# ScalarE is allowed to take the weights' low words, and every step gets a new place and a new engine choice

## The chip, the cores and the metric

The kernel runs on one core of one Trainium2 chip. The metric is device microseconds (us) of one execution; the figure shown is the median of three runs. The engines are TensorE (PE, with its weight loads as PEld), VectorE (DVE), ScalarE (ACT), GpSimd (POOL) and SyncE (SP), which issues nearly all DMAs.

## The reference

Attention over 8 batch elements, 8 heads, 576 positions and 64 channels. All scores that lie more than tau under the maximum of their row are dropped before the softmax. A gated feed-forward layer follows, which mixes each position with the one before it:

```python
scores = scale * np.matmul(q, k.transpose(0, 1, 3, 2))
scores = np.where(scores >= np.max(scores, axis=-1, keepdims=True) - tau, scores, -1e9)
attn = softmax(scores); x = np.matmul(attn, v)      # heads side by side: 8 x 576 x 512
xk = mu_k * x + (1 - mu_k) * x_prev; xr = mu_r * x + (1 - mu_r) * x_prev
out = sigmoid(xr @ w_r) * (np.maximum(xk @ w_k, 0.0) ** 2 @ w_v)
```

The three weight matrices arrive as 64-bit floats (512x1024, 1024x512 and 512x512).

## The kernel before, in words

**Jobs and units.** A job is a pair of heads of one batch element. There are 36: the first batch element is cut into two halves (jobs 0 to 7), and each later batch element has four jobs (8 to 11, 12 to 15 and so on). A job has up to four units of two times 128 query rows and one unit for the last 64 positions. For every block of 128 rows and 576 keys, `softmax` makes four steps: PE writes the scores to PSUM (tile `s`, two of them); DVE takes the negated maximum of each row (L740); a small step derives the row's threshold (L748 on ACT, L756 on DVE or L761 on POOL); ACT takes the exponential (L768); DVE masks it by the threshold and sums it (L776). The block is then turned (by PE at L830 for the early jobs, by DVE and DMA for the later ones), copied out of PSUM by `evict` (L845 on ACT or L846 on DVE), and multiplied by v in `attend` (PE, L1017). I call this last step a job's product.

**Feed-forward.** When all jobs of a batch element are done, `ffn_chunk` handles 256 positions at a time: L1211 (xk by w_k), L1262 (xr by w_r) and L1285 (squared activations by w_v) on PE, with ACT, POOL and DVE steps between them.

**Weights.** `weight` turns each of the 20 pieces of 128x512 64-bit floats (8 of w_k, 4 of w_r, 8 of w_v) into 32-bit floats, and then into a high and a low part. POOL clamps the high words (L444), and ACT scales them into a buffer (L451). DVE shifts the low words right by 29, which leaves three bits, and writes these to a PSUM tile (L459). DVE ors the sign in (L467), and shifts the buffer left by three and ors the PSUM tile in (L477). A copy on ACT or POOL makes the high part (L487 or L491) and POOL subtracts it (L496).

**Order.** No loop and no planner run on the chip. The kernel text adds 5647 steps in program order. A table of two-character digits, PLACES, gives each step its place, and a string, PICKS, gives one digit to each step that may run on several engines. The steps are issued in the order of the table, so each engine has a fixed queue and waits at each instruction for what it needs. 21 steps of dummy transposes on PE (L1378) are among them. PSUM holds two score tiles `s` and four general tiles `w`, and the low words' bits use one of these four.

Of the kernel before, what the change touches and what calls it, by code (L numbers as in the profile page):

```python
# [22 lines left out]
    "!(!!!$!#!+!,!o%x!*!)!%!&!1!=!r!}$0$C$>$G$^%C%m!.!c!n#)#1#=#E#H!w#g$U&)&9&](Z(t!2!]#G#Q#a#w$M&>!0#b&4(*(9(B(S(~#+#m#v",  # L23
    "&p&y(%(z)+!`&Q)&)1)H)^*,*7#@$B(`(b(p({*(*A#L$;)w*4*D*N*T*b%[&J)s)f)y*%*9*Z!f$)*B*S*d*n*v*{$E&~*Y*y*~+)+0+8$])j*x+.+3",
    "+A+K+R!e#>+G+E+T+e-<-H$?&[,|.1.A.N.q/$#4$F+p,C,Q,X.E/Y%d(0+c+[+o+|,*,=(l+`-a-N-i-u-~.)#Z.4/T/M/]/e/j/o*)-e0$0*060<0G",
    "0L!-!P#l!>!<!C!E!F!Q!?!A!B!D!S!V!x#!!_!k!X!q!^#&!T!O![!b!d!j!U!W!Y!a!l!~#3#8!s##!y#(#-#0#:#I#N#d#h#p!@#,$Z!i!m!p!u!t",
    "!z!v!|!{#%#*#D#M#O#<#B#6#J#T#[#$#.#/#7#2#9#5#C#;#F#W#}$1$:$!$+#j#s#R#Y$J$N$O$S$V$[!/!R%W#A#U#K#V#P#X#`#f#c#i#{#~$I$T",
    "#n#x$($5$2$@#r#_#z$%$#$-#e#q#k#u$8$=$z$~$g$x$,$<$`$c%,%2%4%F%K%c!Z#?&<#S#]#t$9$4#|#o$$$.$6#y$D$K$H$P$&$3$/$7$Y${%+%B",
    "$p$t$l%8$k$n$A$X$L$R$Q$W$b$i$h$o%b%o%|&!$r%$%&%:%=%N&,&/&1&6&:&K$_%3%U%g*K%9%I%V&c()(8(^)T)q(J(i)S){*0*6*=*F*L*Q*U*W",
    "*e+D+m+r,),1,4,:,k,o,r,{-:-@.:.T*@*J*O*]*a*g*q*z+,+w-k.v-v-z-}.+.U.^.c.e.m.w/</C+4+;+>+M+V*u*|+(+C+Q,Y/Q/_/b/h0P0^0b",  # L30
    "1E1L1_0y0}1%11191G1u1{2%2T$*$e(3$m$w$}%#%(%E%S%@%L$a$d$f$j$s$q$u%7%<%M%]%f&$%}%j%p%s$v$y$|%%%!%-%*%0%)%1%.%5%?%G%P%_",
    "%r&&%T%`&E&G%>%D%6%;%H%X%R%Y%A%O%J%Q%n%v&i&l%l%w%~&?%e%k&x(#(&(-(/(T(Y%/%h))%{&+&0&H&X&T&2&8&B%Z%^%a%i%u%q%z&C&N&R&`",
    "&Z&g&d&k&n&u%t%y&%&(&#&*&-&3&.&5&7&=&f($(1(6&A&U&M&_&h&t&;&@&F&I&D&S&L&V&P&Y&W&b&q&z(A(X&{(2&s&|(](d(o(s(y(|)%);)=&O",
    "(()z(.(5(<(C(H(M(=(W(e&^&a&e&j&r&w(+(Q(v)>)L(I).(n(E(K(L(4(7&m&o(>(D(F(N&v&}(!(,(m(u)#),(_(g(:(?(j(x(V(a(;(@(h(q(r)$",
# [263 lines left out]
def tile_threshold_attention_then_rwkv_ffn(  # L298
# [17 lines left out]
    P = 128  # L316
# [94 lines left out]
    def weight(j, name, w, c, f, key, wait):  # L411
# [8 lines left out]
        def t():  # L420
            return xT[1].get()[:, col, 1 : 1 + 512]
# [7 lines left out]
        def high():  # L429
# [1022 lines left out]
```

## Time and profile before

| | us |
|---|---|
| median of 3 runs | 916.03 (915.87 to 916.19) |
| the profiled execution's own time | 915.72 |
| its span, first to last instruction | 914.0 |
| DMA busy share in the window from 75 to 150 us | 0.40 |

Busy time is the union of an engine's instruction intervals. PE's intervals are modelled and overlap, so a full row of PE does not mean that PE runs at its peak. A number of the form x24 counts instructions. The granted clock is full over the whole span in the page's slices.

### The profile page before, as it was taken

The page shows a single profiled execution, that of the slowest core. Times are in us where ns is not written, and L with a number is a line of the kernel's source. Part 1 is how long each engine was busy: PE and PEld are TensorE (multiplying, and loading weights), DVE is VectorE, ACT ScalarE, POOL GpSimd, SP SyncE. Part 2 cuts the span into 40 slices and gives each one's busy share as a digit, 9 for nine tenths or more (in the row PEclk, how much of TensorE's full clock was granted, in tenths as well). Part 3 has the DMA queues.
Part 4 walks back from the last instruction along what each step waited for, and adds up shares of the span by engine and source line. Part 5 has one row for each costly group of instructions (what it writes and reads, how often), then busy time and mean ns, then how long its engine had stood idle before and what let it go on. Part 6 is the DMA issues. An engine that isn't in the chain of part 4 may idle for free.

```text
span 914.0 us, 17624 instructions
## 1 busy us (share of the span) xinstructions
PE 902.3 (99%) x5970; PEld 744.1 (81%) x5970; DVE 715.5 (78%) x1615; ACT 598.5 (65%) x1154; POOL 666.5 (73%) x824
## 2 busy tenths in 40 slices
PE   8999999999999999999999999999999999999997
PEld 6677877797878887988887978888889888879986
DVE  7999999998878898988889988888888777701131
ACT  6789999778675767565755475757686666434211
POOL 1789988886774967786977686867687868577742
PEclk9999999999999999999999999999999999999999
DMA  8767333499989999899987979999898887630001
GB/s 332 276 217 246 105 106 119 145 305 308 334 296 311 313 320 322 301 323 313 299 297 272 315 252 321 305 321 320 296 321 291 281 310 261 238 131 24 24 24 23
DMA packets 146249, 226.60 MB, mean 248 GB/s; under 512 B 20080, under 2 KB 82672, under 8 KB 146160
## 3 DMA queue, kind: packets, MB, share of 16 engines
q1 hardware_dynamic: 146016, 225.49, 73.1%
q8 instruction: 47, 0.77, 0.4%
q14 instruction: 42, 0.34, 0.1%
q10 hardware_dynamic: 144, 0.00, 0.0%
HBM read 108.27 MB, written 73.14 MB: 198 GB/s over the span
## 4 chain that ended last, share of the span: by engine, by line
PE 84%; DVE 9%; ACT 4%; issue 1%; POOL 1%; ACTq 0%; DVEq 0%; POOLq 0%
PE w L1211 21%; PE w L1285 20%; PE w L1017 15%; PE s L656 12%; PE w L1262 9%; DVE p L776 3%; DVE sm L740 3%; PE s L628 3%; PE w L830 2%; PE s L639 2%; ACT p L768 2%; ACT pm L845 1%; DVE pt L865 1%; PE w L1378 0%; DVE r L1161 0%
## 5 line engine op out<-in xcount | busy, mean ns | idle before, releaser
L768 ACT ACTIVATE p<-s,sm 128x576 f32<-128x576 f32 x288 | 209.6, 738 | 122.8 <-DVE sm L740 100.0
L776 DVE SCALAR_TENSOR_TENSOR p<-s,sm,p 128x576 f32<-128x576 f32 x288 | 230.9, 811 | 32.4 <-ACT p L768 19.7
L740 DVE TENSOR_REDUCE sm<-s 128x1 f32<-128x576 f32 x288 | 213.2, 750 | 42.4 <-PE s L656 30.4
L1211 PE MATMUL w<-xk,wk 128*128 128x256 f32 x1728 | 227.5, 281 | 0.0
L1211 PEld LDWEIGHTS w<-xk,wk 128*128 128x128 f32 x1728 | 215.8, 188 | 4.1 <-issue 1.7
L1285 PE MATMUL w<-wv,k 128*128 128x512 f32 x864 | 218.0, 395 | 0.0
L1285 PEld LDWEIGHTS w<-wv,k 128*128 128x128 f32 x864 | 157.6, 188 | 31.2 <-ACT raw L529 0.4
L1017 PE MATMUL w<-pm,v 128*64 128x256 f32 (+1 forms) x1280 | 164.9, 409 | 0.0
L1017 PEld LDWEIGHTS w<-pm,v 128*64 128x64 f32 x1280 | 88.1, 137 | 64.0 <-issue 5.8
L865 DVE STREAM_TRANSPOSE pt<-p 128x1024 f32<-128x1024 f32 x96 | 117.8, 1228 | 8.0 <-POOL p L812 5.0
L812 POOL TENSOR_SCALAR p<-p,sm 128x576 f32<-128x576 f32 x119 | 89.2, 753 | 39.0 <-DVE sm L801 36.7
L1243 POOL TENSOR_TENSOR k<-r,k 128x512 fp32r<-128x512 f32 x72 | 93.0, 1294 | 31.0 <-ACT k L1224 28.4
L816 ACT ACTIVATE p<-p,sm 128x576 f32<-128x576 f32 x133 | 101.3, 771 | 20.2 <-DVE sm L801 19.8
L1262 PE MATMUL w<-wr,xk 128*128 128x512 f32 x432 | 112.4, 395 | 0.0
L656 PE MATMUL s<-st 128*128 128x288 f32 x480 | 107.9, 308 | 1.9 <-DVE p L776 1.6
L567 POOL TENSOR_TENSOR hl<-raw,hl 128x640 fp32r<-128x640 f32 (+1 forms) x64 | 97.9, 1539 | 14.3 <-ACT hl L550 7.8
L656 PE MATMUL s<-st,st 128*128 128x288 f32 x480 | 102.2, 296 | 0.0
L656 PEld LDWEIGHTS s<-st 128*128 128x128 f32 x480 | 78.3, 189 | 20.4 <-DVE p L776 8.3
L1262 PEld LDWEIGHTS w<-wr,xk 128*128 128x128 f32 x432 | 77.5, 188 | 13.8
L656 PEld LDWEIGHTS s<-st,st 128*128 128x128 f32 x480 | 77.2, 188 | 1.9
L1220 ACT ACTIVATE r<-r 128x512 f32<-128x512 f32 x72 | 45.4, 631 | 34.8 <-DVE r L1219 33.7
L1291 DVE TENSOR_TENSOR sg<-w,sg 128x512 f32<-128x512 f32 x36 | 24.0, 680 | 44.8 <-PE w L1285 40.9
(93 smaller groups left out, 1129.3 us busy)
## 6 DMA issues: line engine op xcount, KB each, us to landing
far<-pt SPq DMA_DIRECT2D x96, 576.0 KB, 4.2
pm<-far SPq DMA_DIRECT2D x48, 1152.0 KB, 7.3
st<-hl SPq DMA_DIRECT2D x64, 288.0 KB, 3.9
raw<-in_qk SPq DMA_DIRECT2D x28, 640.0 KB, 5.0
st<-hl SPq DMA_DIRECT2D x56, 256.0 KB, 3.8
v<-in_v SPq DMA_DIRECT2D x36, 320.0 KB, 4.0
st<-hl SPq DMA_DIRECT2D x64, 144.0 KB, 3.3
out<-sg SPq DMA_DIRECT2D x32, 256.0 KB, 4.0
```

The source lines that it names most:

```text
L567: lambda cs=cs: G.tensor_tensor(hl.get()[:, 1, cs], raw.get()[:, cs], hl.get()[:, 0, cs].bitcast(F32), op=ALU.subtract),
L656: PE.matmul(ss[y].get()[:, z, 0:HS], l.get()[:, c * P : (c + 1) * P], r[:, z * HS : (z + 1) * HS], start=(j == 0), stop=(j == 1),)
L740: lambda sv=sv, col=col: V.tensor_reduce(col(0), sv(), axis=AX.XY, op=ALU.max, negate=True),
L768: lambda sv=sv, pv=pv, col=col: A.activation(pv(), sv(), AF.Exp, bias=col(0)),
L776: lambda sv=sv, pv=pv, col=col: V.scalar_tensor_tensor(pv(), sv(), col(1), pv(), op0=ALU.is_ge, op1=ALU.mult, accum_out=col(2)),
L816: alt=[("ACT", 0.667, lambda y=y: A.activation(half(y), half(y), AF.Copy, scale=sm.get()[:, 3, y : y + 1]))],
L865: V.transpose(o, x)
L1017: PE.matmul(o[g].get()[hs, 0 : n[g]], vt.get()[:, c, hs], pt, start=(c == 0), stop=(c == 4))
L1211: PE.matmul(h.get()[:, f], l, r, start=(ct == 0 and i == 0), stop=(ct == NCT - 1 and i == 2))
L1243: lambda r=r, js=js: G.tensor_tensor(k2.get()[:, 1, js], r.get().rearrange("p (a b) -> p a b", a=2), k2.get()[:, 0, js].bitcast(F32), op=A ...
L1262: PE.matmul(z.get(), l, r, start=(ct == 0 and i == 0), stop=(ct == NCT - 1 and i == 2))
L1285: PE.matmul(vps.get(), l, r, start=(ft == 0 and i == 0), stop=(ft == NFT - 1 and i == 2))
```

## The change

The step that brings the low words to three bits (the shift by 29 on DVE, L459) gets a second form: one ACTIVATE on ScalarE that reads the 32-bit words as integers, multiplies them by 2^-29 x 0.936 and writes an integer to the PSUM tile, with a rounding where the shift cuts off. This adds one digit to PICKS for each of the 20 pieces (1282 digits become 1302). Both tables are replaced. The steps are the same 5647 and the dummy transposes still number 21.

```diff
+L_SCALE = 2.0**-29 * 0.936
...
         add(
             "DVE",
             0.6,
             lambda: V.tensor_scalar(bu(), words.get()[:, :, 0], 29, None, op0=ALU.logical_shift_right),
             reads=[(words, 0)],
             writes=[bits],
             key=key,
+            alt=[("ACT", 0.57, lambda: A.activation(bu(), words.get()[:, :, 0], AF.Copy, scale=L_SCALE))],
         )
...
 PLACES = (   # all lines replaced: the place of each of 5647 steps
...
 PICKS = (    # all lines replaced, 20 digits more: the engine of each step that has a choice
```

Read off the tables, over the whole kernel (steps, not instructions):

| step | engines before | engines after |
|---|---|---|
| low words to three bits | DVE 20 | ACT 18, DVE 2 |
| row threshold (L748, L756, L761) | ACT 93, DVE 117, POOL 78 | ACT 65, DVE 142, POOL 81 |
| copies out of PSUM (L845, L846) | ACT 176, DVE 56 | ACT 176, DVE 56 |
| all steps | DVE 1271, ACT 1123, POOL 774 | DVE 1278, ACT 1111, POOL 779 |

Ahead of two products, in the queue of each engine up to the last step on which the product rests (steps):

| | DVE | ACT | POOL |
|---|---|---|---|
| job 10's product, before to after | 277 to 288 | 308 to 289 | 147 to 150 |
| job 12's product, before to after | 354 to 370 | 376 to 366 | 198 to 190 |
| of these ahead of job 12: low words | 20 to 2 | 0 to 18 | - |
| row threshold | 26 to 48 | 35 to 12 | - |
| copies of 128x128 | 7 to 17 | 45 to 35 | - |
| copies of 128x256 | 3 to 4 | 13 to 12 | - |

The order of PE's queue changes by a few places at most points (about 5 on average, 103 at most). Its dense matmuls keep their number.

## Rows read from the trace of the kernel before

**Rows 1.** Page part 1: engine, busy us, share of the span, instructions.
```profile
PE 902.3 (99%) x5970; PEld 744.1 (81%) x5970; DVE 715.5 (78%) x1615; ACT 598.5 (65%) x1154; POOL 666.5 (73%) x824
```
**Rows 2.** Windows: stretch, length; busy us (instructions) of each engine; clock, DMA share, GB/s.
```profile
0.00:25.00 25.00, 22.40 (x128) 16.07 (x129) 18.11 (x43) 16.08 (x35) 6.42 (x17) 1.00 0.90 339
25.00:75.00 50.00, 48.72 (x356) 34.75 (x356) 47.95 (x115) 42.23 (x103) 39.96 (x55) 1.00 0.73 241
75.00:150.00 75.00, 73.75 (x549) 59.24 (x546) 73.44 (x175) 72.81 (x164) 67.47 (x81) 1.00 0.40 140
150.00:209.00 59.00, 58.74 (x408) 49.37 (x408) 56.37 (x130) 45.81 (x92) 50.97 (x66) 1.00 0.64 213
600.00:813.00 213.00, 212.85 (x1409) 178.08 (x1407) 163.44 (x353) 134.78 (x238) 153.74 (x195) 1.00 0.86 289
813.00:914.00 101.00, 96.38 (x575) 82.91 (x574) 18.83 (x49) 26.73 (x44) 54.04 (x62) 1.00 0.07 22
```
**Rows 3.** The chain that ended last, shares by line, from 75 to 150 us.
```profile
by line: DVE sm L740 15.5%; DVE p L776 14.4%; ACT p L768 8.3%; ACT pm L845 6.8%; PE w L1211 6.7%; PE w L830 6.2%; issue 6.0%; DVE w L459 4.9%; PE s L656 4.6%; DVE xT L477 4.1%; DVE w L467 4.0%; PE w L1017 3.8%; ACT p L816 2.8%; PE s L628 1.
```
**Rows 4.** The same chain from 209 to 813 us.
```profile
by line: PE w L1211 24.4%; PE w L1285 22.3%; PE w L1017 18.2%; PE s L656 15.3%; PE w L1262 11.0%; PE s L628 3.1%; issue 0.8%; DVE sm L740 0.8%; DVE p L776 0.8%; DVE r L1161 0.6%; DVE pt L865 0.6%; POOL hl L567 0.5%; POOL p L812 0.2%; POOL x
```
**Rows 5.** Groups of DVE, 0 to 209 us: count, busy us, mean ns, idle before.
```profile
L756 DVE TENSOR_SCALAR sm<-sm,small 128x1 f32<-128x1 f32 x29 | 5.9, 208 | 0.1
L459 DVE TENSOR_SCALAR w<-wk 128x512 uint32<-128x512 uint32 x8 | 5.5, 688 | 0.0
L459 DVE TENSOR_SCALAR w<-wv 128x512 uint32<-128x512 uint32 x8 | 5.5, 688 | 0.0
L459 DVE TENSOR_SCALAR w<-wr 128x512 uint32<-128x512 uint32 x4 | 2.7, 685 | 0.0
L846 DVE COPY pm<-w 128x128 f32<-128x128 f32 x5 | 1.4, 285 | 0.0
L846 DVE COPY pm<-w 128x256 f32<-128x256 f32 x3 | 1.2, 415 | 0.5 <-ACT pm L845 0.5
```
**Rows 6.** Groups of ACT, 0 to 209 us.
```profile
L748 ACT ACTIVATE sm<-sm,small 128x1 f32<-128x1 f32 x35 | 10.3, 295 | 4.5 <-DVE sm L740 4.3
L845 ACT ACTIVATE pm<-w 128x128 f32<-128x128 f32 x27 | 7.6, 281 | 3.0 <-PE w L830 3.0
L451 ACT ACTIVATE xT<-wv 128x512 f32<-128x512 f32 x8 | 5.6, 696 | 0.0
L1219 ACT ACTIVATE r<-w 128x512 f32<-128x512 f32 x6 | 3.5, 591 | 0.4 <-PE w L1211 0.4
L451 ACT ACTIVATE xT<-wr 128x512 f32<-128x512 f32 x4 | 2.6, 672 | 0.0
L550 ACT ACTIVATE hl<-raw 128x1280 fp32r<-128x1280 f32 x2 | 2.5, 1272 | 0.0
```
**Rows 7.** Waits of ACT from 25 to 209 us: total, times, longest.
```profile
ACT p L768 <- DVE sm L740: 9.5, 11, 1.9
```
**Rows 8.** The chain in order of time: the products of jobs 10, 12 and 13.
```profile
156.48 5.00 PE w L1017 x40
...
209.07 5.00 PE w L1017 x40
...
233.89 5.00 PE w L1017 x40
```
**Rows 9.** Timeline: the longest wait of PE behind 209 us.
```profile
490.82 0.53 PE L656 MATMUL s<-st 128*128 128x288 f32 x2 [1.38 <-DVE p L776]
```
**Rows 10.** The chain in order of time: the end.
```profile
898.23 11.16 PE w L1285 x48
...
909.41 0.69 DVE sg L1291
```

More of the change, by code (lines that the diff above doesn't have):

```diff
@@ new lines @@
+    "0m!.!S#O!;!=!>!D!A!E!C!G!H!T!U!X!c!o!_!g![!l!e#-!V!R!^!f!d!i!W!Y!Z!b!k!m!v!~!|#,!t!w!x#!#2#4#9#G#J#d!?#($Q!h!n!p!r!s",
+    "!y!u!}!{#$#7#T$)$,#M#X#i#s#<#]###)#+#6#.#8#3#D#:#E#H#b$&$.#g#j#m#y#k#x$3$5$E$J$L$S!<#U%X#A#Q#I#R#N#V#a#e#f#l$-$D$P$Z",
+    "#r#z$+$>$/$9#t#`#}$%$$$0#h#n#o#u$I$g$n%%$f$u$k$y$R$m%2%4%G%J%P%Z!]#%&A#*#;#B#F#p$4#Y#C#S$:#|$B$G$F$K$*$7$2$<$T$t%.%>",
+    "${%#$q$|$^$b$A$U$H$O$M$X$a$j$h$o%d%t%y%|%*%9%&%5%C%O&-&0&4&:&<&O$Y%@%M&G(^%[%i&V&`&q&z(/(p*U(&)*)O)u*&*+*-*9*F*H*M*O",
@@ new lines @@
+    "*Y+S+v,),2,6,:,m,p,v,w,z-D-r-z.#*Z*_*h*l*o*q*t*v+)+G.6.E-S-X-}.!.*.,...7.N.d/,/1+>+A+K+Q+h*~+(+9+H+Y1&/H/L/d/l0c0u1$",
+    "131U1h0{1?1D1p1v2%2*202K2Z#w$V(6$l%!$r%,$s%A%T%F%L$_$c$e$i$v$p$w%:%<&P&X%h&%%w%W%u%n$~%$$x$z%)%/%0%7$}%-%(%1%K%Q%V%e",
+    "&!&+&H&L%Y%_%?%D%8%;%H%S%U%a%B%N%I%R&)&3&W&d%p%x%v%~%l%q&}(#()(+(1(h(l%3%g)7%}&*&8&I&a&Y&2&9&N%]%b%c%k%s%r%z&&&,&?&D",
+    "&v(;(A&x&|(.%m%{&$&(&#&1&/&7&.&6&5&=&E&c(:(C&b&o&^&f&T&Z&K&M&@&C&S&_&]&e&J&Q&R&[(@(Q(Y(a&r&w(B(T&m&s(q(u(w),)0)<)>&U",
@@ new lines @@
+    "(0)t(5(?(H(I(=(V(N(D(]&g&h&k&{($(%(,(3(Z(o(z(G(b(e)$)2)-(4(7&n&y(<(K(F(M(!(-(*(2(t)A)F)J(j(y(J(O(_(~(S(W(9(>([(m(f(s",
+    "(E(P(L(R)&);)M)Z):)?)6)E)P)V)`*;*1(d)9+{)C)K)[)c)S)k)])N)h(`(c(g(n(x(v({)T)a){*!)X)o)m)}*6*2(})#)%)+)()1)/)5).)4)3)B",
+    "*%*/*Q*T)D)H)U)s*B*E)=)@)I)Q)R)n)^)q)Y)_)d)i***0*R*]*7*<*C*K*j*w+d,*+|-b*.,@,c,k,s-M-p.X/>/h/}1b2G2j0_111Y1l2^2{3&3*",
+    "353R3j3p3}4/464831323@3U3_3e3i3n4?4B4E4K2P2T2V2`2c2e2i2t2x33373K2l2o2r3$303F3J3W3Z3b3f3k3A3M3t3x3~4O4i5(565U5Y4T4s4y",
@@ new lines @@
+    "5!5/5=5C5G5l684Y4_4n595K5Q5V5]5f5m)y*g-a+#+F+T+O+s+n+f+i+`)r)v)z)~*4*,*5*a+$+M+]+t+e+b+x+u*=*?*#*3*D*W*P*X*>*I*G*N*d",
+    "*i*m*s*y+&+3+[+++6*b*e*V*[*p*z*x+%*c*{*n*|+;+D+^+l,/,;+y,%,.,4,F,b,Z+/+1+,+5+4+=+?+L+:+C+B+I+_+k+}+q,=,?,,,0,9,J+W+Z",
+    "+P+X+a+p+j+r+g,!,+,1,H,N,R,],Y,_,h,x,g,t-*-L,$,W/=,d,|-,-.,n-B-G-P-V+~,&,(,-,7,5,<,G,O,S,i-9-7,}-2--,>,A,B,E,D,K,L,Q",
+    ",I,T,P,U-!-0-6-=-@-H-F-O-Q-Y,a,e,[,`,j,q,r,y,f,o,l,u-5-8->-E-Z-c-`-h-R-e.H.c.Z,~-#-%-(-&-1-/-4-+-:-3-;-A-J-W-d-s-~-w",
@@ new lines @@
+    "./-k-o-<-?-I-N-C-K-U-]-T-_-[-g-m-x.%-{.2.O.1.@.=.A.|/:-^.80l.M.i._.}.w/6/%.V/+-l-q-v.$.3.+.4.?.C.F.a.p.r.`.n/&-f-i.&",
+    ".(-n-y-u-|.-.9.5.;.K.Q.U.T.e.t.g.k.o/3.<.>.B.G.D.I.L.S.J.R.].f.s.v/$.z/5/S/D/I/;/B/~050>.Y.^.u.y.b.j.h.l/!/-/(/./9/F",
+    "/J/O/[/c/Y/u/X/].m.q///2.x.~/#/*/7/@/E/K/R/V/a/Z/k0&/i/p/v/y020@/C/x2I0!0+03040,0a0]0e0w/8/</A/G/M/N/W/o0*0I0Z151,0X",
+    "0v0t/_/b/Q/T/e/q/j/r/`/f/g/m0$0(0:000B0J0G0S0F0H/z/|/s/w0#0/0-01/{0%07090=0A0D0C0K0P0`0p0N0U1P1o1}0<0?0O0R0E0M0L0Q0T",
@@ new lines @@
+    "0[0Y0b0h0|1%1#1;1e1-171:1M0V0W0q0s0^0g0d0i0x0}0~1(1L1T1s1`1~2+1g1j1{22272u2J2n4[5E6)3!3T3v3z4>4U4q5;5>4e4l4r5%6_6b6j",
+    "6n6q6y6z72777>7B7F5p5t636=6@6C6H6M6Q6X6^6c5h5j676I6R6Z6t767M7Q7X7]6e6i6w7#7(7,7C7O7j7t7y7~7G7J7Y7_7f7.7:7?7T7[7}828G",
+    "8K8P8T8j8q8~9*9G8-888>8B8]8a8g8u9/9i4R5P5a6$7|8D5g6B7a7e8&819!9;9T868A8Q8k9h9p:0:2:4:C:F:N:R:X:]:f9%9(9+919495989=9D",
+    "9V9W9g:+:7:<:A:H:K:`:a:m:s:y;#9.9f9m9t9x9{9~:#:-:1:::@:[:r:};(;3:U:d:i:w;0;w;7;;;[;^;j;|<#<0<L<r;1;n;t<-<8<=<C<J<]<c",
@@ new lines @@
+    "0;0k5&191E1N1y1]212<25280j0n0o0r0z0y1!1*1.10161@1=2k1d1t2U2N3%1)1+12181/141>1A1<1C1B1F1I1Q1[1^1f1n1r1J1O1G1H1R1_1V1a",
+    "1K1W1S1Z1w1z2&2$2,2>2B3+1i1k1c1m1q1|1x2#1u2(2!2)2.2=2@2D2W2d2g2-2/2426232;2:2A292E2?2F2M2Q2]2S2v2|3#3G4.5*4u4I1X2C65",
+    "2_3]2s3o2q3a3{3w4$2O2Y2[2a2m2h2p363B3E3L3V3S534}4f4Q5)4W2H2L2w2~2R2b2X2f3(3.3-343:3<3D3?3^3I3h2y2z3;3=2}3,3)3/3C3O3H",
+    "3P3`4%4,4)47454:4^38393c3d3>3N3Q3X3l3r3s3y4(4+41444G4=4P3Y3[3|4!3g3q3m3u4-4342494D4F4Z4d4o4t4w5@5w6V6A6}4<4j834~5.5H",
@@ L121 @@
+    "`u`n`o`p`q`ya(a+a.a/a2`r`t`z`|`}`~a$a&a*a-`:`d`ka%`j`v`w`x`{a#aIa!a)a,a>aCaDaFaHaJaKaMaPaTa]aaa1a6a;a=a@aAaGaLaNaRaV",
+    "aXa0a3a4a5a7a8a9a:a<a?aBaEaOaQaSaUaYaZa[a^a`acaeagaWa_aiajalabadafahanapasauavawaxaza|a~b$b&b%akamaoaqarataya{a}b#b!",
+    "!2!3!4!5!6!7!8!9!:!J!K!L!M!N!O!P!Q#1#?#@#_",
 )
 PICKS = (
[L123 to L124 removed]
@@ L135 @@
+    "10010011001000111110101101",
 )
 W_SCALE = 2.0**-112
+L_SCALE = 2.0**-29 * 0.936
 W_MAX = 2.0 ** (0x8F - 127) * (1 + 0x6FFFFF / 2.0**23)
```

188 lines of the change are left out of this document (78 added, 110 removed).

## The prediction

> **What bounds the kernel now.** I read the busy times first. PE stands at 99% of the span [rows 1], which seems to leave nothing to an edit on other engines. Its intervals are modelled and overlap, though, so I went on to the windows and to the chain of waits.
>
> The windows show two regimes [rows 2]. From 25 to 150 us DVE is busy for 47.95 + 73.44 = 121.4 of 125 us (97%), ACT for 115.0 (92%) and POOL for 107.4 (86%). From 75 to 150 us alone DVE has 1.6 us left and ACT 2.2. From 600 to 813 us DVE is at 77% and ACT at 63%.
>
> The chain agrees. From 75 to 150 us its largest entries are DVE's row maximum (15.5%), DVE's mask (14.4%) and ACT's exponential (8.3%); the matmul lines shown come to about 21% [rows 3]. From 209 to 813 us PE's lines make up 94% [rows 4]. So PE sets the time behind about 209 us, and DVE, with ACT close behind it, sets it ahead of that. What the early part gains stays gained if PE's queue behind it finds its operands ready.
>
> The Trainium skill ("Perfetto Trace Analysis", Identifying the Most-Contended Engine) says that a matmul's busy share is a poor measure of how near TensorE is to its limit, and that the share of the weight loads is a better one. The trace bears this out: from 25 to 75 us PE is 97% busy while its loads fill 34.75 of 50 us (70%); from 600 to 813 us they fill 178.08 of 213 (84%) [rows 2]. By the busy share alone the change could give at most the 12 us of PE's idle time and most likely nothing (my second rival); by the loads the early part has room.
>
> **The low words.** Of 20 passes, 18 leave DVE. Each takes 0.688 us there by its three rows (8 + 8 + 4 pieces) [rows 5], so DVE loses 18 x 0.688 = 12.4 us, all of it ahead of 209 us. L459 itself holds 4.9% of the chain from 75 to 150 us, 3.7 us [rows 3].
>
> On ACT the new pass reads 128x512 integers from SBUF and writes PSUM, which no row shows. From below I take the pass of 512 columns out of PSUM, 0.591 us; from above the pass of 1280 columns, 1.272 us; the nearest rows are the passes of the same tile's other words, 0.672 and 0.696 us [rows 6]. I take 0.67, so ACT gains 18 x 0.67 = 12.1 us (10.6 to 22.9).
>
> The Trainium skill ("ScalarE: Activation LUTs", Rules for kernel authors) speaks against this move: multiplies and the like belong on VectorE, which it calls up to three times faster for 16-bit data. The rows of 32-bit words show no such gap, 0.688 us on DVE beside 0.672 to 0.696 on ACT [rows 5, 6]. If it did hold here, 18 passes of 2.06 us would be 37 us on ACT, and this is the extreme of my last rival.
>
> The PSUM tile that takes the bits is one of four that PE uses as well. In both orders the or and the shift on DVE follow within a few PE steps, so I cost its holding time at nothing. If that cover is gone, PE waits for a `w` tile, as much as 1.4 us at a time by the largest wait of PE [rows 9].
>
> **The exchange that comes with it.** The tables hand work back. I counted the steps in each queue ahead of job 12's product, which starts at 209.07 us [rows 8], and multiplied by the rows.
>
> - DVE: 22 more row thresholds x 0.208 = +4.6; ten more copies of 128x128 x 0.285 = +2.9; one of 128x256, +0.4 [rows 5]. With small terms +0.1, DVE's sum is -12.4 + 8.0 = -4.4 us.
> - ACT: 23 fewer thresholds x 0.295 = -6.8; ten fewer copies x 0.281 = -2.8 and one of 0.4 [rows 6]; other choices (copies of the weights' high parts to POOL, scaling and squared activations to ACT) +2.1 by the mean durations of their groups. Sum: +12.1 - 10.0 + 2.1 = +4.2 us.
> - POOL: -3.3 us by the same count, 8 steps fewer. PE's own work ahead of this product differs by less than 1 us.
>
> Ahead of job 10's product (156.48 us [rows 8]) the same count gives DVE -7.3 and ACT -1.4: some softmax rows of later jobs, two maxima among them, now stand behind it. So in the tightest stretch both engines have less queued in front of the product, and ACT takes its added load early and late, where it has room. From 0 to 75 us it is idle for 75 - 58.3 = 16.7 us, and from 150 to 209 us for 13.2 us [rows 2].
>
> A second gain is in the threshold: where DVE makes it, the mask behind it waits for no other engine. ACT waits 9.5 us for the row maximum between 25 and 209 us [rows 7], and with L748 in its queue it can wait for it twice per row block. I leave this out of the sum, since exp still waits for the same maximum.
>
> **Behind 209 us** the order and the engines are reshuffled too. PE has its long waits behind it, but for one of 1.38 us at 490.82, on a mask that frees a score tile [rows 9]. A new order can remove this or make another like it: 0, plus or minus 1.5. The end stays: 48 matmuls of w_v close PE's queue, and one multiply and the stores follow [rows 10].
>
> **The sum.** If every microsecond that DVE loses ahead of 209 us came back, the gain would be 4.4 us. DVE is not the pacing engine throughout: it is idle for 6.9 of the first 25 us and 2.6 of the last 59 [rows 2], and ACT gets 4.2 us more. I take 80%: 3.5 us. The profiled execution took 915.72 us, so 912.2. The shown median lies 0.31 higher, so the prediction is 912.5 us. Of the forecast's own range, the lower end is the whole 4.4 plus the 1.4 at 490 us, 910.2, and the upper end is 1.5 us of gain, 914.5.
>
> **Rivals.**
>
> 1. *ACT takes DVE's place as the bound.* From 75 to 150 us ACT is already 97% busy. If its idle time elsewhere can't be used, because it lies in front of row maxima that come too late [rows 7], the 4.2 us that it gains ahead of 209 us lengthen the path: 916.0 + 4.2 = 920.2 us. It decides from the point where ACT's queue ahead of job 10's product grows. For it: the small margin, and 14 of the 18 new passes already ahead of job 7's product, where ACT's count is 3.2 us higher. Against it: ahead of job 10's product the count is 1.4 us lower.
> 2. *No change.* The early gaps of PE come from the latency of the loop of scores, maximum, exponential, mask and turn rather than from DVE's load, and a lighter DVE only waits longer. For it: PE's busy share. Against it: DVE is 98% busy from 75 to 150 us, so it hardly waits. Time 916.0, within 1.8.
> 3. *More than the sum.* Ahead of job 13's product (233.89 us [rows 8]) DVE's count is 8.6 us lower, and ACT's 1.5 us lower. If DVE paces up to there, all of it comes back: 916.0 - 8.6 = 907.4 us. Against it: from 150 to 209 us DVE is at 96% and PE nearly fills its time, so part of that is only work that moved behind the product.
> 4. *The new pass is dear,* near the upper bound of 1.27 us or beyond. ACT then gains 22.9 - 10.0 + 2.1 = 15.0 us against the 10.0 that it has idle from 25 to 150 us, so some 5 us are added: 921 us or more, and with 37 us for the passes far more. That the tables hardly use the pass is excluded: 18 of 20.
>
> **How the numbers follow.** Forecast 0.52, more than the sum 0.11, no change 0.19, ACT as the bound 0.14, the dear pass 0.04. A difference of less than 0.2% (1.8 us) can't be told from none, so faster means below 914.2. Of the forecast's chance 0.05 lies above that. Faster: 0.47 + 0.11 = 0.58. Same: 0.05 + 0.19 = 0.24. Slower: 0.14 + 0.04 = 0.18. The range from 908.5 to 917.0 takes in the forecast, no change and the nearer half of the third rival and leaves out most of the first and the last.
>
> **What would show it.** In the changed kernel's profile the low words' pass should be 18 ACTIVATEs near 0.67 us; one above 1 us is rival 4. Job 10's product should start about 3 us before 156.5 us, and job 12's about 3 to 4 before 209.1. DVE's busy time from 25 to 150 us should stay near 97% while it covers more of the work: falling to 92% with ACT at 97% is rival 1, and both falling is rival 2. Behind 209 us the chain should be PE's as before, and the gain at the end should be the one at job 12; a wait of PE of over 1.5 us there would be what the prediction has left out. I am wrong if job 12's product starts no earlier than before, or if it does and the end doesn't follow.

## The result: 923.8 us, 0.86% slower, and outside the predicted range

The changed kernel takes 923.80 us (median of four, 922.58 to 925.67), the kernel before 916.11 us beside it. The ratio is 1.0086, 95% interval 1.0065 to 1.0107. I forecast 912.5 us and gave "slower" 0.18. The profiled execution took 922.58 us, with a span of 920.8. Of the four, two took 922.58 and 922.74 us with TensorE's granted clock full, and two 924.86 and 925.67 at a mean of 0.998; the late loss below has a part that goes with this.

Lines behind the new pass have moved by two: L740 of before is L742 after, L776 is L778, L768 is L770, L656 is L658, L1161 is L1163. The new pass on ScalarE is L464. The splices and x7 number these lines as before does.

Page part 1 of the changed kernel (engine, busy us, share of the span, instructions), to be laid beside [rows 1]:

```profile
PE 906.6 (98%) x5970; PEld 744.8 (81%) x5970; DVE 715.0 (78%) x1622; ACT 594.9 (65%) x1138; POOL 677.9 (74%) x833
```

Over the span DVE and ACT do about as much as before, POOL 11 us more. The windows of the changed kernel, columns as in [rows 2]:

```profile
25.00:75.00 50.00, 49.34 (x360) 35.80 (x358) 47.31 (x118) 45.49 (x104) 40.49 (x59) 1.00 0.74 248
75.00:150.00 75.00, 73.76 (x540) 58.47 (x538) 71.42 (x182) 71.86 (x153) 67.49 (x78) 1.00 0.37 134
150.00:209.00 59.00, 58.01 (x401) 47.94 (x400) 55.42 (x129) 48.09 (x98) 44.07 (x54) 1.00 0.62 212
400.00:600.00 200.00, 195.58 (x1269) 162.26 (x1268) 172.47 (x386) 129.32 (x236) 151.12 (x184) 1.00 0.88 291
```

From 75 to 150 us DVE's busy time fell from 73.44 to 71.42 us and ACT's from 72.81 to 71.86 [rows 2]: each waits more, and PE gets no further ahead. From 400 to 600 us PE is idle for 4.4 us, against 1.4 in before by the same window there:

```profile
400.00:600.00 200.00, 198.62 (x1288) 165.86 (x1287) 174.81 (x395) 127.72 (x239) 154.73 (x189) 1.00 0.89 298
```

The new pass itself came out at the price that I took. Its line in the changed kernel (durations in ns, shortest, median, longest):

```profile
L464 ACT ACTIVATE w<-wk x8: 639/656/692, 20.1 to 80.7; 128x512 uint32<-128x512 uint32 x8
L464 ACT ACTIVATE w<-wv x6: 626/646/653, 99.9 to 147.5; 128x512 uint32<-128x512 uint32 x6
L464 ACT ACTIVATE w<-wr x4: 646/655/663, 83.4 to 96.8; 128x512 uint32<-128x512 uint32 x4
```

The chain of waits of the changed kernel, first from 75 to 150 us and then from 209 to 813 us, beside [rows 3, 4]:

```profile
by line: PE w L1019 16.1%; PE s L658 12.0%; PE w L832 11.9%; DVE p L778 9.7%; ACT p L770 7.9%; DVE sm L742 6.2%; PE w L1213 5.7%; ACT w L464 4.1%; DVE xT L479 4.1%; ACT pm L847 3.0%; issue 2.7%; DVE w L469 2.4%; ACT r L1222 2.4%; PE s L630 
...
by line: PE w L1213 23.9%; PE w L1287 20.7%; PE w L1019 17.4%; PE s L658 15.6%; PE w L1264 10.7%; PE s L630 2.8%; issue 1.4%; DVE m L1163 1.2%; DVE p L778 1.2%; DVE sm L742 0.8%; POOL k L1245 0.6%; DVE pt L867 0.5%; POOL p L814 0.4%; ACT p 
```

In the early stretch DVE's maximum went from 15.5% to 6.2% and its mask from 14.4% to 9.7%, with PE's lines in their place. DVE's share of the chain shrank as I meant it to, and the time did not follow. Behind 209 us a line of DVE appears that [rows 4] show as L1161 with 0.6%: the mixing of positions, L1163, 1.2%.

Chain in order of time, the products of jobs 10 and 13 of the changed kernel, and the timeline's row for job 12's:

```profile
157.51 5.00 PE w L1019 x40
...
236.64 5.00 PE w L1019 x40
```

```profile
210.60 5.07 PE L1019 MATMUL w<-pm,v 128*64 128x320 f32 x40
```

For jobs 10, 12 and 13 that is 1.0, 1.5 and 2.8 us later than before [rows 8], where I had the first two 3 to 4 us earlier. By the sentence that I had set myself, the prediction is wrong at its first test.

To see where each microsecond goes I laid PE's steps of both traces side by side: at the same amount of PE's own work (868 us in both), how much later than in before does PE start? This is worked out from all of PE's rows, so it is my table and not a view of the profile; small values of either sign (under about 0.7) are differences in the first 25 us.

```
PE's own work ahead, us     60    110   130   150   180   340   440   460   480   860
starts in before at, us   73.8  133.1 156.2 178.1 210.1 373.4 474.6 496.4 516.8 901.1
changed kernel later by   -0.5   -0.7  +1.0  +3.1  +2.3  +2.1  +3.7  +4.1  +6.8  +6.9
```

Nothing is gained or lost up to 133 us, where 16 of the 18 passes have moved. Then 2.3 to 3 us are lost by 178 us and 4.7 more between 373 and 517 us, 1.6 of these by 475 us and 3.1 behind it. These are two losses, and the experiments take them one by one.

### The profile page after: what moved, and what is told of

Read it like the earlier page. It is cut to its first block, busy times and chain, and to the rows that moved or that the text cites. A ratio compares the mean times of both kernels' runs of the same rounds, so it can differ in the third digit from the quotient of the medians.

```text
span 920.8 us, 17622 instructions
## 1 busy us (share of the span) xinstructions
PE 906.6 (98%) x5970; PEld 744.8 (81%) x5970; DVE 715.0 (78%) x1622; ACT 594.9 (65%) x1138; POOL 677.9 (74%) x833
## 4 chain that ended last, share of the span: by engine, by line
PE 84%; DVE 8%; ACT 5%; issue 2%; POOL 1%; DVEq 0%; ACTq 0%; POOLq 0%
PE w L1213 20%; PE w L1287 19%; PE w L1019 15%; PE s L658 13%; PE w L1264 9%; DVE p L778 3%; PE w L832 3%; PE s L630 2%; DVE sm L742 2%; ACT p L770 2%; PE s L641 1%; DVE pt L867 1%; DVE m L1163 1%; ACT pm L847 1%; PE w L1380 1%
## 5 line engine op out<-in xcount | busy, mean ns | idle before, releaser
L770 ACT ACTIVATE p<-s,sm 128x576 f32<-128x576 f32 x288 | 210.0, 740 | 131.8 <-DVE sm L742 103.2
L778 DVE SCALAR_TENSOR_TENSOR p<-s,sm,p 128x576 f32<-128x576 f32 x288 | 231.0, 811 | 29.5 <-ACT p L770 14.9
L742 DVE TENSOR_REDUCE sm<-s 128x1 f32<-128x576 f32 x288 | 212.5, 749 | 48.5 <-PE s L658 36.4
L1287 PE MATMUL w<-wv,k 128*128 128x512 f32 x864 | 220.3, 395 | 0.0
L814 POOL TENSOR_SCALAR p<-p,sm 128x576 f32<-128x576 f32 x133 | 99.3, 752 | 39.8 <-DVE sm L803 35.7
L658 PE MATMUL s<-st 128*128 128x288 f32 x480 | 109.0, 311 | 6.7 <-DVE p L778 5.9
L658 PEld LDWEIGHTS s<-st 128*128 128x128 f32 x480 | 77.6, 188 | 32.2 <-DVE p L778 18.0
L658 PE MATMUL s<-st,st 128*128 128x288 f32 x480 | 101.7, 296 | 0.0
L818 ACT ACTIVATE p<-p,sm 128x576 f32<-128x576 f32 x119 | 90.6, 772 | 14.1 <-DVE sm L803 13.7
L658 PEld LDWEIGHTS s<-st,st 128*128 128x128 f32 x480 | 77.2, 188 | 2.5 <-issue 0.3
L1221 ACT ACTIVATE r<-w 128x512 f32<-128x512 f32 x49 | 29.2, 597 | 45.5 <-PE w L1213 36.3
```

What stands on the lines that cost most here:

```text
L658: PE.matmul(ss[y].get()[:, z, 0:HS], l.get()[:, c * P : (c + 1) * P], r[:, z * HS : (z + 1) * HS], start=(j == 0), stop=(j == 1),)
L742: lambda sv=sv, col=col: V.tensor_reduce(col(0), sv(), axis=AX.XY, op=ALU.max, negate=True),
L770: lambda sv=sv, pv=pv, col=col: A.activation(pv(), sv(), AF.Exp, bias=col(0)),
L778: lambda sv=sv, pv=pv, col=col: V.scalar_tensor_tensor(pv(), sv(), col(1), pv(), op0=ALU.is_ge, op1=ALU.mult, accum_out=col(2)),
L814: lambda y=y: G.tensor_scalar(half(y), half(y), sm.get()[:, 3, y : y + 1], 0.0, op0=ALU.mult, op1=ALU.add),
L1287: PE.matmul(vps.get(), l, r, start=(ft == 0 and i == 0), stop=(ft == NFT - 1 and i == 2))
```

## Experiments

All were timed in five rounds beside the kernel before, whose median was 915.56 to 916.31 us in them. One thing comes along unasked: which buffer of a tile a step gets is worked out from the places and from the planned durations of the engines chosen. Going by the kernels' text, another step stands ahead in the same `w` tile for 4 of its 381 uses in x2, 10 in w1, 17 in x1, 20 in x3 and 42 in x4, each against the kernel that it is derived from, and the splices share out several kinds of tiles anew. The z and y kernels and x7 keep every buffer.

### The passes alone, and the new order without them

```diff
 x1_low_back: the changed kernel
-    18 low-word passes on ACT
+    18 low-word passes on DVE
 x2_low_only: the kernel before
-    20 low-word passes on DVE
+    18 low-word passes on ACT
```

> The changed kernel with the 18 passes over the low words back on VectorE, at the same places of the order; all other engines and all places stay as changed. Theory A (ScalarE pays for the passes): ScalarE loses 18 x 0.65 = 11.7 us of work in the first 165 us, and the 2 to 3 us that TensorE loses between 133 and 189 us go; about 920 to 921 us. Theory B (the places in the queues decide, whatever the engine of the low words): VectorE is again full and gets 12.4 us more on top of what the exchange gave it; 925 to 930 us, and the loss at 490 to 515 us stays.

> The kernel before with the same 18 passes on ScalarE and nothing else changed (its own order, its other engine choices). Theory A: ScalarE, 97% busy from 75 to 150 us, gets 8 us there that nothing takes away: 918 to 922 us. Theory B: the pass itself is harmless, VectorE is freed of 12.4 us where it was full: 912 to 916 us.

x1 took 931.91 us, ratio 1.0167 (1.0151 to 1.0183), and x2 922.42 us, 1.0069 (1.0055 to 1.0083). x1 lies above both ranges that I had expected of it, x2 just above the nearer one. So the 18 passes on ACT cost 6.2 us in before's order and save 8.1 us in the changed one. x2's loss arises ahead of 156 us. Its window from 75 to 150 us:

```profile
75.00:150.00 75.00, 71.95 (x520) 56.05 (x520) 64.60 (x151) 73.69 (x171) 64.39 (x77) 1.00 0.38 135
```

DVE has 10 of 75 us free there and ACT, busy for 73.69, is the one without room. The rows agree with the reading by loads in this: adding to an engine without room costs. It does not follow that taking away pays.

### Taking load away from one engine

z2 is the kernel before with the low-word pass on DVE cut to 8 of its 512 columns, and with an `and` in place of the last `or`, so that the numbers stay finite. Its weights mean nothing, and only its time is read. z1 is the changed kernel with the passes on ACT and DVE cut in the same way. w1 is z2 with its 35 early row thresholds of ACT moved to DVE.

```diff
-V.tensor_scalar(bu(), words.get()[:, :, 0], 29, ...)
+V.tensor_scalar(bu()[:, 0:8], words.get()[:, 0:8, 0], 29, ...)
...
-    tu(), tu(), 3, bu(), op0=ALU.logical_shift_left, op1=ALU.bitwise_or
+    tu(), tu(), 3, bu(), op0=ALU.logical_shift_left, op1=ALU.bitwise_and
```

> The kernel before with VectorE's low-word passes (L459) cut to 8 of 512 columns, and the last step combining with an and in place of an or so that its numbers stay finite: the other low words are left out. It takes about 20 x 0.55 = 11 us from VectorE and gives nothing to ScalarE. My forecast's reason (VectorE's load sets the time ahead of 209 us) expects most of it back: 906 to 910 us. The rival reason, that the table's order was fitted to these engines and durations and each engine waits at places the others set, expects little: 913 to 917 us.

> The changed kernel with the low-word passes, 18 on ScalarE and 2 on VectorE, cut to 8 columns in the same way. It takes 18 x 0.42 = 7.6 us from ScalarE. If ScalarE's load paces the changed kernel ahead of 190 us (my first rival), 4 to 7 us come back and the early loss of 2 to 3 us is gone: 916 to 919 us. If the places decide: 922 to 924 us.

> The kernel before with the cut low-word passes of z2_before_short (VectorE has room, 11 us of the low words are left out) and the 35 row thresholds that ScalarE made ahead of 200 us (L748, 0.295 us) put on VectorE (L756, 0.208 us); places unchanged. If ScalarE paces the kernel before ahead of 150 us, its 10.3 us less give back 3 to 6 us: 910 to 913 us. If no engine's load sets the time there, but the waits at the places of the order, as z2 suggests for VectorE: 914 to 917 us.

z2: 916.67 us, 1.0009 (1.0000 to 1.0018). z1: 923.80 us, 1.0085 (1.0071 to 1.0099), the changed kernel's own time, though each of ACT's 18 passes took 0.18 us in place of 0.65, 8.5 us in all. w1: 919.57 us, 1.0040 (1.0026 to 1.0054). The windows from 75 to 150 us of z2 and then of z1:

```profile
75.00:150.00 75.00, 73.73 (x550) 59.35 (x547) 68.73 (x173) 72.87 (x165) 67.36 (x82) 1.00 0.41 141
```

```profile
75.00:150.00 75.00, 74.00 (x542) 58.85 (x541) 71.38 (x182) 67.98 (x152) 67.79 (x79) 1.00 0.37 134
```

In z2 a pass takes 0.16 us in place of 0.69, so DVE has some 10 us less to do, and its busy time falls by 4.7 us in this window alone. PE starts 0.4 us earlier at 210 us, and the end does not move. The chain of z2 in that window and DVE's waits in it show where the time went:

```profile
by line: ACT p L768 12.7%; ACT pm L845 10.8%; PE w L1211 10.2%; PE w L830 9.7%; PE s L656 9.0%; DVE p L776 6.1%; DVE sm L740 5.8%; ACT p L816 4.9%; PE w L1017 4.5%; issue 3.5%; PE s L628 2.5%; ACT xT L451 2.3%; ACT r L1220 2.1%; PE w L1262 
```

```profile
DVE sm L740 <- PE s L656: 1.7, 4, 0.6
DVE p L776 <- ACT p L768: 1.2, 4, 0.5
```

DVE's maximum and mask fall from 29.9% of the chain [rows 3] to 11.9%, and the exponential, the copies and PE take their shares. DVE now waits for score tiles and exponentials. w1 carries it further: against before ACT has 35 x 0.295 = 10.3 us less [rows 6] and DVE still some 3 us less, and the kernel is slower by 0.40%, 3.7 us, 2.3 of it by 133 us. What makes it slower was not tested: the thresholds at their new places in DVE's queue, or the ten `w` tiles. A busy share of 98% was a true reading of DVE's queue and a wrong one of the limit: by the chain, PE (which turns and multiplies), DVE and ACT pace this stretch in turn.

### Order and engine choices, one without the other

```diff
 x4_order_only: PLACES of the changed kernel, PICKS of before
 x3_picks_only: PLACES of before, PICKS of the changed kernel
```

> The changed order with the engine choices of the kernel before (low words on VectorE too). If a table of places is fitted to its own engine choices, the mixed pair loses more than the change itself: 925 to 940 us, early above all. If the order alone carries the loss of the change: 922 to 925 us. If the engine choices carry it: 915 to 918 us.

> The order before with all the changed engine choices (18 low words on ScalarE, fewer thresholds and copies there). If places and engines are fitted to each other: 925 to 940 us. If the choices alone carry the loss of the change: 921 to 925 us. If the exchange of work undoes the cost that x2_low_only showed for the passes alone (6 us): about 916 to 918 us.

961.12 us, 1.0500 (1.0486 to 1.0514), and 964.81 us, 1.0534 (1.0519 to 1.0548), both above the 925 to 940 that I had expected at most. Either half of the change costs 46 to 49 us, and the two together 7.7. The differences in the two tables are not a sum of small edits, each with its own price, and my count of instructions ahead of a product treated them so.

### Where the early loss belongs

Splices at a point of PE's work: up to the seam every step has the place and engine of one kernel, behind it of the other.

```diff
 x5_early_after: changed kernel to 333 us, then before
 v1_after_to_127: changed kernel to 127 us, then before
 v2_after_to_158: changed kernel to 158 us, then before
 v3_middle_after: before to 127 us, changed kernel to 235 us, then before
 x6_late_after:   before to 333 us, then the changed kernel
```

> A splice: the changed order and engine choices for the steps that the kernel before issues in its first 333 us, and those of the kernel before from there on. If the loss has two places, an early one of 2 to 3 us between 133 and 189 us and a late one of 4 us between 440 and 515 us, this keeps the early one alone: 918 to 919.5 us, without the late waits. If the loss is spread or comes from one cause, it keeps either all (922 and more) or none (916) of it.

> The kernel before, but everything that it issues in its first 127 us takes the order and the engines of the changed kernel (942 steps, 16 of the 18 passes on ScalarE among them); the order and engines of before follow. Theory A: the passes and the changed kernel's early order cost nothing by themselves, and the early loss of 2.3 us arises from the placing between 133 and 189 us: then this kernel takes 915.5 to 916.5 us, and PE's start times differ from before's by less than 0.7 us from 150 us on. Theory B: what ScalarE takes on early leaves it behind, and the loss shows later whatever order follows: 918 to 919 us. Theory C: a seam between two orders costs something of its own, of either sign up to 2 us, shown as waits of PE within 15 us behind the seam.

> The same with the seam at 158 us (1175 steps and 19 passes' steps, 17 or 18 of them on ScalarE). Theory A with the loss spread evenly between 133 and 189 us: half of it, 917 to 917.5 us; if it all stems from the placing ahead of 158 us, 918 to 919 as with the seam at 333 us (918.98). Theory B: 918 to 919. Theory C: any time between 914 and 919, with PE's waits close behind the seam.

> The kernel before with only the stretch that it issues from 127 to about 235 us in the changed kernel's order and engines; the passes ahead of 127 us stay on VectorE as in before. Theory A: the placing of this stretch alone brings the loss of 2.3 to 3 us: 918 to 919 us. Theory B: without the passes on ScalarE the loss is gone: 915.5 to 916.5 us. Theory C: as above, both seams.

> The kernel before up to 333 us and the changed kernel's order and engines from there. If the late loss belongs to the placing behind 400 us alone: nothing lost early, 4 to 4.6 us lost between 400 and 517 us, 920 to 921 us. If it needs the changed kernel's early loss to arise (arriving 2 us later puts the mixing beside other work of GpSimd): 916 to 917.5 us.

```
                      median us  ratio (95%)               later than before at PE's work of
                                                            110   130   150   180   440   480   860
x5 to 333 us            918.98   1.0028 (1.0019 to 1.0037)  -0.3  +1.4  +3.5  +2.7  +2.8  +1.5  +1.9
v1 to 127 us            918.91   1.0028 (1.0018 to 1.0039)  +2.5  +2.5  +2.5  +2.5  +2.7  +2.8  +4.5
v2 to 158 us            918.17   1.0021 (1.0012 to 1.0029)  +0.1  +1.9  +2.3  +2.3  +2.1  +2.1  +2.5
v3 127 to 235 us        921.21   1.0054 (1.0042 to 1.0066)  +1.2  +2.8  +4.9  +4.1  +5.0  +5.0  +5.3
x6 from 333 us          923.01   1.0066 (1.0054 to 1.0078)  +0.4  +0.4  +0.4  +0.4  +2.7  +7.0  +7.5
```

x5 keeps the early loss and has none of the late one. x6 has no early loss and a late one of 6.7 us by its times and 6.6 by the table, against 4.7 in the changed kernel and the 4 to 4.6 that I had expected. So the late loss does not come from arriving late. Its size can't be laid beside the changed kernel's as it stands: in x6's profiled execution the granted clock falls for 3.4 us behind the long wait of PE, and in the changed kernel's it does not (the rows are shown with the late loss). With the clock full x6 took 921.14 us, in one execution, 4.8 above the kernel before beside it, the changed kernel 922.58 and 922.74, some 6.5 above, and x5 918.98, 2.7 above. So each loss costs by itself, and within some 1 us the two add up.

For the early loss v3 decides against what ScalarE took on ahead of it: with those passes on DVE the stretch still loses, and more in all (921.21 us) than the 918 to 919 that I had expected, its seam included. The waits of PE behind 140 us, in the changed kernel and then in v3 (start, duration, instruction, in brackets the idle time before it and what ended it):

```profile
143.02 0.53 PE L658 MATMUL s<-st 128*128 128x288 f32 x2 [0.24 <-DVE p L778]
147.50 0.52 PE L658 MATMUL s<-st 128*128 128x288 f32 x2 [0.32 <-DVE p L778]
166.12 0.53 PE L658 MATMUL s<-st 128*128 128x288 f32 x2 [0.58 <-DVE p L778]
```

```profile
129.45 0.30 PE L830 MATMUL w<-ident,p 128*128 128x128 f32 x1 [1.48 <-ACT pm L845]
144.83 0.53 PE L656 MATMUL s<-st 128*128 128x288 f32 x2 [0.24 <-DVE p L776]
149.30 0.53 PE L656 MATMUL s<-st 128*128 128x288 f32 x2 [0.31 <-DVE p L776]
167.91 0.53 PE L656 MATMUL s<-st 128*128 128x288 f32 x2 [0.57 <-DVE p L776]
```

The last three rows of v3 are the same three waits, of the same lengths. They belong to the placing of this stretch. The first row of v3 is its seam. v1 too pays at its seam and nothing more until 517 us: at 133 us it is 2.5 us behind before, where x5, whose queues of PE, DVE and ACT are the same up to 122 us, is 0.3 ahead. That is theory C of v1's expectation, not B. A seam's price can't be told from that of the order behind it, so v1 does not clear the opening, but the changed kernel itself does, with -0.7 us at 133 us.

What such a wait is made of stands in the changed kernel's timeline of DVE and ACT ahead of the third:

```profile
163.28 0.76 DVE L742 TENSOR_REDUCE sm<-s 128x1 f32<-128x576 f32 x1 [0.31 <-PE s L658]
...
163.82 0.28 ACT L847 ACTIVATE pm<-w 128x128 f32<-128x128 f32 x1
163.95 0.68 DVE L848 COPY pm<-w 128x512 f32<-128x512 f32 x1
164.39 0.74 ACT L770 ACTIVATE p<-s,sm 128x576 f32<-128x576 f32 x1 [0.30 <-PE w L832]
...
165.24 0.82 DVE L778 SCALAR_TENSOR_TENSOR p<-s,sm,p 128x576 f32<-128x576 f32 x1 [0.61 <-ACT p L770]
```

The maximum waits 0.31 us for PE's scores, the exponential starts 0.35 us after the maximum, the mask waits 0.61 us for it, and then PE waits 0.58 us for the mask to free the score tile. I read this round, 163.28 to 166.06 us, as bound by its latency and by what stands between its steps in the queues. This is the mechanism of my second rival, in a stretch where every engine looked full. The three waits listed make 1.1 of the 2.3 to 3 us. The rest is spread over delays too short to be listed, and which placements make them stays open.

### The late loss: mixing on DVE beside GpSimd

In the feed-forward of the batch elements' last 64 positions, which comes twice (near 490 and near 875 us), the mixing of each position with the one before it is done on DVE, in blocks of eight instructions in a row, each with two inputs in SBUF. Their rows between 484 and 510 us, in before and in the changed kernel:

```profile
485.75 4.16 DVE L1161 SCALAR_TENSOR_TENSOR r<-m,mu_sb,xE 128x64 f32<-128x64 f32 x8
491.70 2.04 DVE L1161 SCALAR_TENSOR_TENSOR m<-m,mu_sb,xE 128x64 f32<-128x64 f32 x8
499.04 1.65 DVE L1161 SCALAR_TENSOR_TENSOR r<-m,mu_sb,xE 128x64 f32<-128x64 f32 x8
500.90 2.44 DVE L1161 SCALAR_TENSOR_TENSOR m<-m,mu_sb,xE 128x64 f32<-128x64 f32 x8
```

```profile
487.78 4.29 DVE L1163 SCALAR_TENSOR_TENSOR m<-m,mu_sb,xE 128x64 f32<-128x64 f32 x8
501.56 1.64 DVE L1163 SCALAR_TENSOR_TENSOR r<-m,mu_sb,xE 128x64 f32<-128x64 f32 x8
509.19 5.21 DVE L1163 SCALAR_TENSOR_TENSOR m<-m,mu_sb,xE 128x64 f32<-128x64 f32 x8
```

The same work takes 1.64 us or 5.21 us. What GpSimd does beside the last block, and PE's two waits, in the changed kernel:

```profile
509.21 1.57 POOL L569 TENSOR_TENSOR hl<-raw,hl 128x640 fp32r<-128x640 f32 x1 [1.35 <-ACT sm L798]
510.75 1.05 POOL L1275 TENSOR_SCALAR sg<-sg 128x1024 f32<-128x1024 f32 x1
511.76 1.57 POOL L569 TENSOR_TENSOR hl<-raw,hl 128x640 fp32r<-128x640 f32 x1
```

```profile
493.24 0.53 PE L658 MATMUL s<-st 128*128 128x288 f32 x2 [1.69 <-DVE p L778]
...
515.25 0.53 PE L658 MATMUL s<-st 128*128 128x288 f32 x2 [2.17 <-DVE p L778]
```

Behind each slow block the mask stands in DVE's queue, and PE waits for the score tile that it frees. [Rows 9] show one such wait in before, 1.38 us, behind the block of 4.16 us; the changed kernel has two, 3.9 us together. That is 2.5 us more of the 3.1 lost behind 475 us. The 1.6 us lost from 373 to 475 us lie ahead of the first block (480.7 us) and are not the mixing's; where they come from stays open.

Four kernels test this. y3 takes the first end chunk's mixing off DVE in the changed kernel, and y1 that of both chunks; y2 is y1's edit in before; x7 only moves the two slow blocks behind the next masks.

```diff
 y1, y2, y3 (y3 only where b0 == 0):
-V.scalar_tensor_tensor(d[y], diff[y], mu[y], prv, op0=mult, op1=add)
+A.activation(d[:, y], diff[:, y], AF.Copy, scale=mu[y])
+G.tensor_tensor(d, d, prv, op=add)
 x7_after_mix_late: the places of two blocks, behind the masks that followed them
```

> The changed kernel with the mixing taken off VectorE as in y1_after_mix_off, but only for the first of its two occurrences (488 and 509 us); the second, at 875 us, where the feed-forward waited for GpSimd in y1, stays as it was. If the two held-up blocks are the late loss, the 3 us that y1 won between 480 and 520 us stay without the 2 us that it lost at the end: 919 to 921 us. If not: 922 us or more.

> The changed kernel with the mixing of the last 64 positions taken off VectorE: ScalarE multiplies by mu (two instructions) and GpSimd adds (four), in place of the eight two-input instructions of L1163, which took from 1.64 us with GpSimd idle beside them to 5.21 us with GpSimd busy for 4.2 us. If these held-up blocks are the late loss, TensorE's waits at 491 and 513 us go and 3 to 5 us come back: 918.5 to 920.5 us. If they only stand where VectorE is short of time anyway, or GpSimd becomes late instead, under 1.5 us: 922 us or more.

> The same edit on the kernel before, whose blocks took 4.16, 2.04, 1.65 and 2.44 us and whose one late wait of TensorE is 1.4 us at 490.8 us: if the blocks cause it, 1.3 to 2 us are gained, 914 to 915 us; otherwise 916 us or more.

> The changed kernel with two of the eight-instruction mixing blocks of the feed-forward of the last 64 positions (VectorE, L1163, 4.3 and 5.2 us) moved in VectorE's queue behind the masks that they stood ahead of at 488 and 509 us (one copy on ScalarE that needs the block moves with it). Theory B: TensorE's waits of 1.7 and 2.2 us for these masks go and 3 to 4 us come back: 919 to 920 us. Theory A: no change, 922.6 us or more, since nothing of the low words is touched.

y3: 919.58 us, 1.0044 (1.0031 to 1.0056). It is 4.0 us above the kernel before beside it, where the changed kernel was 7.7 above, so 3.7 us of the loss are back. Its two waits:

```profile
492.93 0.53 PE L658 MATMUL s<-st 128*128 128x288 f32 x2 [0.22 <-DVE p L778]
513.15 0.53 PE L658 MATMUL s<-st 128*128 128x288 f32 x2 [0.33 <-DVE p L778]
```

They shrink from 3.9 to 0.6 us, by 3.3. y1 took 923.50 us, 1.0085 (1.0071 to 1.0099), where I had expected 918.5 to 920.5: what it wins here it loses elsewhere, 1 us by 373 us, with a wait for a DMA at 243 us, and 2 us at the second chunk's own place near 875 us, where PE waits for GpSimd. y2 took 917.52 us, 1.0018 (1.0009 to 1.0027), where I had expected 914 to 915: it is 1.0 us ahead of before at 496 us and 0.6 behind at 517. Between the two DVE waits 2.78 us for GpSimd's scaling of a block (L812, 504.55 us), and PE 1.45 us for the mask behind it (507.81 us). So the mixing moved to GpSimd has a price of its own.

x7 took 925.16 us, 1.0088 (1.0072 to 1.0104), where I had expected 919 to 920. The first block that it moved still met GpSimd, the second hardly did:

```profile
490.72 5.45 DVE L1161 SCALAR_TENSOR_TENSOR m<-m,mu_sb,xE 128x64 f32<-128x64 f32 x8
514.80 1.83 DVE L1161 SCALAR_TENSOR_TENSOR m<-m,mu_sb,xE 128x64 f32<-128x64 f32 x8
```

The first takes 5.45 us, with GpSimd busy for 4.98 of them, and PE waits 2.92 us behind it. The second takes 1.83 us, with GpSimd busy for 0.38, and the wait of 2.17 us is gone; another of 1.47 us has come at 520.98 us, behind no slow block. So the mixing is slow wherever GpSimd is busy, and the cure is a place where GpSimd rests, or another engine; merely standing behind the mask is none.

**What else the long wait costs.** z1 has the changed kernel's two blocks and two waits (1.69 and 2.16 us). In it TensorE's granted clock falls to half, 1.2 GHz, from 517.0 to 520.4 us, 1.5 us after the second wait ends. In the changed kernel's profiled execution it stays full behind the same wait. The windows from 517.00 to 520.30 us of z1 and then of the changed kernel (the value of 0.50 or 1.00 is the granted clock):

```profile
517.00:520.30 3.30, 3.30 (x9) 2.51 (x9) 3.16 (x8) 0.83 (x2) 3.17 (x3) 0.50 0.44 165
517.00:520.30 3.30, 3.30 (x16) 2.34 (x14) 3.16 (x10) 0.83 (x2) 3.00 (x3) 1.00 0.43 158
```

At the same amount of PE's work z1 and x6 each lose 3.9 us between 496 and 517 us, the changed kernel 2.7, so the fall costs some 1.2 us (an estimate, worked out like the table above). x1, x3, x4 and x6 have such a stretch of 3.4 us too, at a wait of 2.2 to 3.2 us; x7 kept its clock behind 2.92 us. No trace without a wait of over 2 us has one ahead of the last few us of its span. All five executions of y3 kept a mean clock of 0.999 or more. With the clock full the changed kernel is, in two executions, some 6.5 us above before, and y3 4.0. By these 2.5 of the 3.7 us are the mixing itself, and the rest goes with the clock. That the wait brings the fall is read from these traces; no run tests it alone.

No kernel tried here is faster than before.

## Why the prediction was wrong, point by point

**The step that failed** is the first: "DVE, with ACT close behind it, sets it ahead of that", and its use in the sum, 80% of DVE's 4.4 us. z2 takes 10 us from DVE, more than twice that, and gives nothing (916.67 us), and z1 takes 8.5 us from ACT and gives nothing (923.80 us). In its place the runs show a loop through PE, DVE and ACT in which each is nearly full and each waits in turn. In z2 the chain's share that left DVE went to ACT and PE. The chain's largest entry names what came last in one execution of one order; what stands directly behind it is not in the chain.

**The working behind it**, steps counted ahead of a product, assumed that order is neutral. x3 and x4 show order and engine choice fitted to each other, to the tune of 46 to 49 us. A count did not price an edit to a fixed order either: z2 counts 10 us less on DVE and is no faster.

**The low words.** I took 0.67 us a pass, the rows show 0.65. The pass was not dear: rival 4 falls, and no wait of PE up to 210 us is put down to the PSUM tile's holding, which I had at nothing.

**Behind 209 us** I put 0, plus or minus 1.5. It was +4.6 us in the profiled execution, some 3 of them behind two blocks of DVE that GpSimd held up, and more in the executions in which the clock fell. I had the one wait of 1.38 us in view [rows 9], called it removable, and did not look at the block ahead of it, which took 4.16 us where another took 1.65 in the same trace. That row alone would have told me that a reshuffle at this place can cost more than 1.5 us. The end itself stayed PE's, as written.

**Rivals.** The dear pass (921 us or more, 0.04) had the nearest number, by luck: the pass took 0.65 us. ACT as the bound (920.2 us, 0.14) came next and has the wrong mechanism here: job 12's product did start late and ACT's share from 25 to 150 us did rise, from 92% to 94%, but z1 shows that its load is not the loss. In x2 the rows agree with it: ACT is 98% busy from 75 to 150 us and the loss is early. "No change" named the mechanism of the early part, latency rather than load, but not that a new order can lengthen it by 2 to 3 us. None of the rivals had the late loss. My signs did not tell them apart either: from 25 to 150 us DVE fell from 97% to 95% while ACT rose from 92% to 94%, and from 75 to 150 us both fell.

**The room in TensorE's loads.** I had leaned on the Trainium skill ("Perfetto Trace Analysis", Identifying the Most-Contended Engine) to read room for a gain ahead of 209 us out of TensorE's loads. The shares were as I read them, 70% against 84%; whether PE could have used the difference no run shows, and lightening DVE did not open it.

**The range.** It ended 6.8 us below the result. Its sizes came from counted load alone; what a new order may cost by itself, 2.7 us in x5 and 4.8 to 6.7 in x6, had no term.

## What to carry to other kernels

Where three engines are each over 90% busy and pass tiles to one another, a busy share doesn't name the bound: ask what waits next if that engine were free, and give load taken from one engine no price of its own. A new order has a price of its own, here several microseconds, beside which the counted gain of 4 is small. Look for groups whose duration varies severalfold in the trace, since a reshuffle draws anew from that spread. Where executions of one kernel differ by 2 us, look at the granted clock of each before laying medians side by side.

## What I had not expected of the hardware

Eight L1161 instructions (L1163 after) take 1.64 us with GpSimd idle. Over the traces, with GpSimd's busy time beside them in brackets, blocks took 2.04 (0.81), 2.44 (1.59), 2.89 (2.73), 4.16 (3.91), 5.21 (4.13) and 5.45 us (4.98). Single ones, 0.27 us when free, last about as long as the GpSimd instruction beside them, up to 1.7 us.

The Trainium skill ("SBUF — State Buffer", Who interferes with whom) says that a DVE instruction with two SBUF inputs contends with a GpSimd instruction that reads SBUF, and that in such contention the one issued first keeps the shared ports for its whole instruction. The durations agree with it: a block became up to 3.3 times as long. That GpSimd holds DVE is read from these durations; no run took GpSimd's work away instead of DVE's.

One wait of PE of some 2 us cost more than its own length in some executions: in five of the seven traces with a wait of over 2 us, the granted clock fell to half for 3.4 us at that wait or within 2 us of its end.
